# Local-and-global attention followed by a token and channel mixer: queries in nine blocks of 64, v loaded uncast and kept twice, PSUM banks handed out singly, and engine orders made by a list scheduler inside the kernel

## The chip, the cores and the metric

The kernel runs on one core of one Trainium2 chip. The metric is the device time of one execution in microseconds (us), lower is better. The engines are TensorE (PE, with its weight loads shown apart as PEld), VectorE (DVE), ScalarE (ACT), GpSimd (POOL) and SyncE (SP). DMAs are issued from the queues of SP, ACT and POOL. Each engine runs its instructions in the order in which the program lists them, and waits on semaphores where an instruction needs another engine's result.

## The reference

Eight batches, eight heads, 576 positions, head dimension 64. Attention is allowed within 32 positions, and to and from 8 global positions. The result, laid out as 576 x 512 for each batch, goes through two mixers with residuals.

```python
# attention: q, k, v are (8, 8, 576, 64) float32
scores = scale * np.matmul(q, k.transpose(0, 1, 3, 2))
mask = np.abs(pos[:, None] - pos[None, :]) <= 32
mask = mask | is_global[:, None] | is_global[None, :]
attn = softmax(np.where(mask, scores, -1e9))
x = (attn @ v).transpose(0, 2, 1, 3).reshape(B, S, 512)
# mixer: w_tok1 (576, 256), w_tok2 (256, 576), w_ch1 (512, 1536), w_ch2 (1536, 512)
h = relu(x.transpose(0, 2, 1) @ w_tok1) @ w_tok2
u = x + h.transpose(0, 2, 1)
out = u + relu(u @ w_ch1) @ w_ch2
```

## The kernel before

**What a batch does.** q and k are loaded as float32 (`lq`, `lk`, the last 64 rows in `lr`), cast to float16 (`cast_qk`, L350, into `qk` and `rn`) and turned so that the head dimension lies on the partitions: in batch 0 by TensorE transposes (`T`, `TE`, L416 to L435), later by DMA transposes on SP's queue (`turn_rest`, `turn`, L363 to L370, into `rawr` and `raw`), after which VectorE puts the columns in order (`order`, L376). `S_` (L437) makes scores for two heads at a time (a "pair", four to a batch). Keys lie in five tiles of 128 that begin 32 positions early, and each key tile meets up to 192 queries and 16 columns for the global positions: 10 matmuls to a pair, two heads at a time in the upper and lower half of the array's rows, of 208 or 144 columns. ScalarE takes the exponential in three instructions a pair (L457, L466, L469), and VectorE multiplies with the mask `bandm` (`SM`, L471: one instruction of 160 elements, two of 1040).

`GK` and `OG` do the global rows, `PV` (L512) multiplies the weights with v in five tiles of 128 queries: for each half of the heads one matmul of 264 columns for the global keys and two of 66 columns for each head, since the queries of a tile meet two key tiles. VectorE divides (L548, L549). `M1` and `M2` are the token mixer (results in `a1` and, with the residual, `u16`), `M3` turns u by DMA (L623, into `uT`), `M4` (L628) and `M5` (L653) are the channel mixer: twelve groups of four 512-column matmuls with a ReLU on ScalarE (L637, `b1`), then four tiles of twelve 512-column matmuls, a sum on VectorE (`osb`, L664) and the store. The last 64 rows of two batches share a tile and are done with the odd batch (`M4l`, `uTl`, L667).

**v.** Batch 0 loads v as float32 from SP and casts it on GpSimd (`castv`). All others load it with a DMA from GpSimd's queue that casts to float16 on the way (`load_v16`, L345). There is one copy, `vsh`, in key tiles of 128.

**PSUM.** Three pools hold the eight banks: two pairs of banks for scores, `GK`, `OG`, `M1` and `M2` (`pss`), one pair for `PV` (`psv`, so that a tile waits until VectorE has divided the one before), two single banks for the channel mixer (`psm`).

**Order.** The program is written under a manual schedule, so engines run what is written in its order. Batch 0 is written out by hand. After it `merge` interleaves two lists: the attention and token mixer of batch b+1 (`sparse`, L671) and the channel mixer of batch b (`dense`, L742), by hand-set weights in us:

```python
add(0.5, lambda p=p: S_(b, p, 0))
add(2.8, lambda p=p: S_(b, p, 1))
...
u = [(0.86, lambda j=j: M4(b, j)) for j in range(NJ)]
```

Of the kernel before, what the change touches and what calls it, by code (L numbers as in the profile page):

```python
# [15 lines left out]
P = 128  # L16
NT = 5
NG = 8
WIN = 32
GW = 2 * NG  # L20
QS = P + GW
EW = 2 * P + GW
VW = 66


def merge(sparse, dense):


    ts, td = sum(c for c, _ in sparse) or 1.0, sum(c for c, _ in dense) or 1.0
    i = j = 0  # L30
    a = d = 0.0
    while i < len(sparse) or j < len(dense):
        if j >= len(dense) or (i < len(sparse) and a / ts <= d / td):
            a += sparse[i][0]
            sparse[i][1]()
            i += 1
        else:
            d += dense[j][0]
            dense[j][1]()
            j += 1  # L40
# [3 lines left out]
def kernel(  # L44
# [24 lines left out]
    mb = ctx.enter_context(tc.tile_pool(name="mb", bufs=2))  # L69
    ob = ctx.enter_context(tc.tile_pool(name="ob", bufs=3))  # L70
    tiny = ctx.enter_context(tc.tile_pool(name="tiny", bufs=4))
# [6 lines left out]
    def pss(shape, dtype=F32, name="s"):  # L78
        return psS.tile(shape, dtype, tag="s", name=name)

    def psv(shape, dtype=F32, name="v"):
        return psV.tile(shape, dtype, tag="v", name=name)

    def psm(shape, dtype=F32, name="m"):
        return psM.tile(shape, dtype, tag="m", name=name)
# [4 lines left out]
    lv = mb.tile([P, NT, H, D], F32, tag="lv", bufs=1, name="lv")  # L90
    qk = const.tile([P, 2, NP, 4, P], F16, name="qk")
    rn = const.tile([P, NP, P], F16, name="rn")
    rawr = const.tile([P, NP, P], F16, name="rawr")
    vsh = [const.tile([P, NT, H, VW], F16, name=f"vsh{i}") for i in range(2)]

    gt32 = global_idx.tensor.bitcast(I32)
# [3 lines left out]
    nc.scalar.dma_start(out=gidx_b.rearrange("p g w -> p (g w)"), in_=bass.AP(tensor=gt32, offset=0, ap=[[0, P], [1, 2 * NG]]))  # L100

    def vrows(c):
        r0 = WIN if c == 0 else 0
        r1 = P - WIN if c == NT - 1 else P
        return r0, r1, P * c - WIN + r0

    def load_qk(b, hs):
        for ten, dst in ((q, lq), (k, lk)):
            nc.sync.dma_start(
                out=dst[:, hs].rearrange("p h i d -> p h (i d)"),  # L110
                in_=ten[b, hs, 0 : S - LAST, :].rearrange("h (p i) d -> p h (i d)", i=4),
            )

    def load_rest(b):
        for t, ten in enumerate((q, k)):
            nc.sync.dma_start(
                out=lr[LAST * t : LAST * t + LAST], in_=ten[b, :, S - LAST : S, :].rearrange("h p d -> p h d")
            )

    def load_v(b):  # L120
        for c in range(NT):
            r0, r1, j0 = vrows(c)
            nc.sync.dma_start(
                out=lv[r0:r1, c], in_=v[b, :, j0 : j0 + (r1 - r0), :].rearrange("h p d -> p h d")
            )

    for p in range(NP):
        load_qk(0, slice(2 * p, 2 * p + 2))
        if p == 0:
            load_rest(0)  # L130
    load_v(0)


# [263 lines left out]
    def G0(p):  # L397

        if p == 0:
            st[0]["pg"] = psm([P, NP, 2, NG], name="pg0")  # L400
# [457 lines left out]
```

## Time and profile before

| | us |
|---|---|
| time, median of 3 runs (lowest, highest) | 353.66 (353.2, 356.38) |
| span of the profiled execution | 353.0 |
| busy: PE, DVE, ACT, POOL | 299.4, 198.7, 163.3, 73.8 |
| HBM read | 36.12 MB, 129 GB/s over the span with 9.44 MB written |

The profiled execution's span is within 0.7 us of the median. A busy PE is not a PE at its peak: a matmul's row lasts longer than the distance to the next one, since they are pipelined. In the views a group's row gives line, engine, operation, tiles and shapes, the count after x, the busy time and the mean of one in ns, and behind the last bar the idle time of the engine ahead of them with what ended it.

### The profile page before, as it was taken

The numbers are of one execution on the slowest core, as the hardware profiler recorded it, in microseconds if no ns is written. First come the engines' busy times: TensorE is split into PE (matmuls) and PEld (weight loads), VectorE is DVE, ScalarE is ACT, GpSimd is POOL, SyncE is SP. The second block draws the span as 40 slices with busy tenths as digits, with TensorE's granted clock in tenths as the row PEclk, the third lists the DMA queues.
The fourth block names the chain that finished last, engine by engine and source line by source line (L and its number), as shares of the span: only waits on it lengthen the run. The fifth ranks groups of instructions, "written<-read, shape, count | busy, mean of one in ns | idle before, by whom it ended". The sixth has DMA issues, their size and how long they took to land.

```text
span 353.0 us, 6305 instructions
## 1 busy us (share of the span) xinstructions
PE 299.4 (85%) x2469; PEld 150.5 (43%) x2469; DVE 198.7 (56%) x407; ACT 163.3 (46%) x292; POOL 73.8 (21%) x113
## 2 busy tenths in 40 slices
PE   1556897893989896889899999798999998898994
PEld 0334433541337442454337434453366433543641
DVE  4898756657174583548545765568354946542021
ACT  2448279050582156806593339415870159012600
POOL 8888663100066200030002100130000000000000
PEclk9999999999799999999999999999999999999999
DMA  6999999996789997596659955595730240025012
GB/s 156 254 289 182 165 154 214 242 118 146 233 184 124 242 193 186 112 279 88 149 104 263 134 126 107 139 268 100 151 62 30 61 119 2 1 75 120 2 59 89
DMA packets 124317, 50.53 MB, mean 143 GB/s; under 512 B 99200, under 2 KB 119552, under 8 KB 124288
## 3 DMA queue, kind: packets, MB, share of 16 engines
q1 hardware_dynamic: 86800, 41.96, 52.1%
q0 software_dynamic: 37200, 8.16, 26.4%
q8 instruction: 19, 0.31, 0.4%
q14 instruction: 10, 0.08, 0.1%
q10 hardware_dynamic: 288, 0.01, 0.0%
HBM read 36.12 MB, written 9.44 MB: 129 GB/s over the span
## 4 chain that ended last, share of the span: by engine, by line
PE 58%; DVE 18%; DMA 9%; ACT 6%; SPq 5%; issue 2%; DVEq 0%; ACTq 0%
PE b1p L634 18%; PE op L660 18%; DMA uT<-u 5%; PE a1p L564 5%; SPq L623 4%; PE s L446 3%; PE pv L519 3%; DVE e_all L479 3%; PE pv L528 3%; DMA raw<-qk 2%; PE pv L533 2%; PE b1lp L647 2%; PE hp L588 2%; DVE x L549 2%; ACT e_all L457 2%
## 5 line engine op out<-in xcount | busy, mean ns | idle before, releaser
L634 PE MATMUL b1p<-uT,wc 128*128 128x512 f16 x384 | 94.5, 386 | 13.1 <-DMA uT<-u 11.3
L660 PE MATMUL op<-wc,b 128*128 128x512 f16 x384 | 90.5, 379 | 0.0
L637 ACT ACTIVATE b<-b1p 128x512 f16<-128x512 f32 x96 | 57.3, 614 | 37.7 <-PE b1p L634 36.2
L634 PEld LDWEIGHTS <-wc 128*128 128x128 f16 x384 | 33.9, 98 | 55.4 <-issue 19.1
L345 POOL DMA_DIRECT2D vsh<-in_v_dram x35 | 29.7, 855 | 115.3 <-PE pv L533 102.0
L660 PEld LDWEIGHTS <-b 128*128 128x128 f16 x384 | 36.2, 98 | 40.7
L457 ACT ACTIVATE e_all<-s 128x832 f16<-128x832 f32 x32 | 27.9, 872 | 38.0 <-PE s L446 25.1
L479 DVE TENSOR_TENSOR e_all<-e_all,bandm 128x1040 f16<-128x1040 f16 x64 | 43.8, 725 | 1.2
L664 DVE TENSOR_TENSOR osb<-u,op 128x512 f32<-128x512 f16 x32 | 21.8, 686 | 33.0 <-PE op L660 32.6
L473 DVE TENSOR_TENSOR eg<-e_all,bandm 128x160 f16<-128x160 f16 x32 | 8.1, 253 | 51.8 <-ACT e_all L469 51.8
L572 ACT ACTIVATE a<-a1p 128x1024 f16<-128x1024 f32 x7 | 7.2, 1024 | 59.5 <-PE a1p L564 59.0
L519 PE MATMUL pv<-rf,lf 128*128 128x264 f16 x80 | 21.5, 283 | 10.1 <-DVE x L549 5.2
L446 PE MATMUL s<-qT,kT 64*128 64x208 f16 (+1 forms) x320 | 23.8, 256 | 6.2 <-DVE qT L393 3.1
L549 DVE TENSOR_TENSOR x<-pv,rr 128x512 f16<-128x512 f32 (+1 forms) x40 | 27.6, 691 | 1.4
L528 PE MATMUL pv<-vsh,e_all 128*128 128x66 f16 x320 | 28.3, 197 | 0.0
L548 DVE RECIPROCAL rr<-pv 128x8 f32<-128x8 f32 (+1 forms) x40 | 8.3, 207 | 35.1 <-PE pv L533 23.7
L528 PEld LDWEIGHTS <-e_all 128*128 128x128 f16 x320 | 24.6, 100 | 4.2 <-issue 2.6
L533 PE MATMUL pv<-vsh,e_all 128*128 128x66 f16 x256 | 24.1, 198 | 0.0
L446 PEld LDWEIGHTS <-kT 64*128 64x128 f16 x320 | 10.8, 97 | 29.7 <-issue 21.7
L466 ACT ACTIVATE e_all<-s 128x576 f16<-128x576 f32 x32 | 21.0, 658 | 3.2 <-PE s L446 3.2
L356 ACT CAST qk<-lq 128x512 f16<-128x512 f32 x28 | 17.3, 618 | 5.4 <-DMA lq<-in_q_dram 5.3
L378 DVE COPY kT<-raw 128x512 f16<-128x512 f16 x28 | 16.7, 595 | 5.5 <-DMA raw<-qk 5.5
(154 smaller groups left out, 343.9 us busy)
## 6 DMA issues: line engine op xcount, KB each, us to landing
out_dram<-osb SPq DMA_DIRECT2D x32, 256.0 KB, 2.4
lq<-in_q_dram SPq DMA_DIRECT2D x7, 1024.0 KB, 6.5
lk<-in_k_dram SPq DMA_DIRECT2D x7, 1024.0 KB, 9.2
wc<-in_moe_w_ch_dram POOLq DMA_DIRECT2D x6, 512.0 KB, 9.9
vsh<-in_v_dram POOLq DMA_DIRECT2D x21, 128.0 KB, 9.5
vsh<-in_v_dram POOLq DMA_DIRECT2D x14, 96.0 KB, 5.4
lq<-in_q_dram SPq DMA_DIRECT2D x4, 256.0 KB, 5.9
lk<-in_k_dram SPq DMA_DIRECT2D x4, 256.0 KB, 5.8
```

The costliest lines, as they stand in the source:

```text
L345: nc.gpsimd.dma_start(out=vsh[b % 2][r0:r1, c, :, 0:D], in_=v[b, :, j0 : j0 + (r1 - r0), :].rearrange("h p d -> p h d"),)
L446: nc.tensor.matmul(ps[:, par, off : off + n], lhsT=kT[r, P * c : P * c + P], rhs=qf[r, lo : lo + n], start=True, stop=True,)
L457: nc.scalar.activation(out=e2[:, :, 1:3, 64:EW], in_=ps[:, :, 0 : 2 * W].rearrange("p h (c x) -> p h c x", c=2), func=AF.Exp, scale=scale)
L479: nc.vector.tensor_mul(out=eh, in0=eh, in1=bandm)
L519: nc.tensor.matmul(ps[:, hf, 0 : NP * VW], lhsT=s["lf"][:, P * tau - sh : P * tau - sh + P], rhs=s["rf"][:, 2 * hf : 2 * hf + 2], start=b ...
L528: nc.tensor.matmul(o, lhsT=e_all[:, h, tau, EW - P - sh : EW - sh], rhs=vsh[b % 2][:, tau, h, :], start=b == 0 and hh == 0, stop=last and ...
L533: nc.tensor.matmul(o, lhsT=e_all[:, h, tau + 1, 0:P], rhs=vsh[b % 2][:, tau + 1, h, :], start=False, stop=last)
L549: nc.vector.tensor_tensor(out=x16s[b % 2][r, tau, :].rearrange("p (f h x) -> p f h x", f=2, h=NP), in0=pq[r, :, :, 0:D], in1=rr[r].unsquee ...
L634: nc.tensor.matmul(ps, lhsT=wc1[:, cc, P * j : P * j + P], rhs=s["uT"][:, cc, :], start=(cc == 0), stop=(cc == 3))
L637: nc.scalar.activation(out=s["b1"][:, j, :], in_=ps, func=AF.Relu)
L660: nc.tensor.matmul(ps, lhsT=w, rhs=wc2[:, j, :], start=(j == 0), stop=(j == NJ - 1))
L664: nc.vector.tensor_add(out=osb, in0=s["u16"][:, tau], in1=ps)
```

## The change

The kernel is largely rewritten. The arithmetic stays the same; what changes is how the attention is cut, who casts, and who decides order and banks.

- **Blocks of 64 (`scores`).** Keys lie in nine blocks of 128 that begin every 64 positions; each block meets just the 64 queries in its middle and 8 global columns: 18 matmuls a pair, each of 72 columns, the two heads again in the two halves of the rows. One exponential for a head (9 x 72 elements), two a pair; one mask multiplication a pair (18 x 72), and one copy of the global columns into `eg`.
- **v.** Loaded as float32 in all batches and cast on GpSimd (`cast_v`). A second copy `vod`, shifted by 64 rows, is made from `vsh` by VectorE copies (`shift_v`), so that odd blocks find their 128 keys in one tile. `PV` (now `values`) keeps its counts.
- **Loads.** k of batch 0 is issued from ACT's queue. From batch 2 on q, k and v are all issued from GpSimd's queue.
- **Turns.** Batches 0 to 2 (`PEB = 3`) turn q, k and u on TensorE, with the evacuation on VectorE or ScalarE; later ones by DMA as before.
- **PSUM.** One tile `bank` of eight banks. Single results take any free bank, scores and `values` an even pair.
- **ReLU** may go to ScalarE or VectorE.
- **Order.** Every step is registered with `op`: engines it may run on with a cost in us, a priority, what it reads and writes. `run` is a list scheduler: it keeps a time for each engine, takes among the ready steps those that start first, and of those within a small look-ahead the one with the lowest priority number. `merge`, `sparse` and `dense` are gone. A function that fills PE's gaps with idle matmuls (`warm`) is there, but is called with a limit of 0.0, which gives none.

```diff
-    psS = ctx.enter_context(tc.tile_pool(name="psS", bufs=2, space=bass.MemoryType.PSUM))
-    psV = ctx.enter_context(tc.tile_pool(name="psV", bufs=1, space=bass.MemoryType.PSUM))
-    psM = ctx.enter_context(tc.tile_pool(name="psM", bufs=2, space=bass.MemoryType.PSUM))
+    bank = psum.tile([P, 8, 512], F32, name="bank")
...
+    def run(free, look, hop, warm_until):
...
+        while ready:
+            cand = {}
+            for i in ready:
...
+                for k, (e, c) in enumerate(o["opts"]):
+                    st = max([free[e], t0] + [f + (hop if x != e else 0.0) for x, f in at[i].items()])
...
+            for e, cs in cand.items():
+                lim = min(x[0] for x in cs) + look[e]
+                x = min((x for x in cs if x[0] <= lim), key=lambda x: (x[1], x[0], x[2]))
...
+            o["fn"](e)
...
+    def scores(b, p, pri):
...
+            for u in range(NB):
+                for z in range(2):
+                    r = slice(64 * z, 64 * z + 64)
+                    nc.tensor.matmul(
+                        ps_tile[keys[z]][:, u // 3, UW * (u % 3) : UW * (u % 3) + UW], lhsT=kT[r, 64 * u : 64 * u + P],
+                        rhs=qT[r, u // 2, UW * (u % 2) : UW * (u % 2) + UW], start=True, stop=True,
+                    )
...
+            op([("A", 0.73)], pri + 1, lambda e, par=par: nc.scalar.activation(
...
+        op([("V", 0.93)], pri + 2, lambda e: nc.vector.tensor_mul(
...
+    def chan1(b, j, pri):
...
+        op([("P", 0.865)], pri, f, r=[("wc1", j // 4)] + [("uT", t) for t in range(4)], ps=[key], new=("M", [key], [P, 512], F32))
+        op([("A", 0.61), ("V", 0.69)], pri - 8, lambda e: relu(e, b1[:, j, :], ps_tile[key]), ps=[key], w=[("b1", j)])
...
-            nc.gpsimd.dma_start(
-                out=vsh[b % 2][r0:r1, c, :, 0:D],
-                in_=v[b, :, j0 : j0 + (r1 - r0), :].rearrange("h p d -> p h d"),
-            )
+                    COPY[e](out=vsh[i][a:z, c, :, 0:D], in_=lv[a:z, c])
...
+                    if lo == 0:
+                        COPY[e](out=vod[i][0:64, cs], in_=vsh[i][64:P, cs])
+                    else:
+                        COPY[e](out=vod[i][64:P, cs], in_=vsh[i][0:64, cs.start + 1 : cs.stop + 1])
...
+    PEB = 3
...
+            gate = [start_of[b - 2]] if b >= 2 else []
```

The scheduler's result is what moves on the engines. Three places follow; a row is line, operation, result<-operands and shape, and x is a repeat.

**ScalarE, the exponentials of one batch beside the ReLUs of the batch before it** (`e_all` is the exponentials' output, `b` the ReLU's, `s`, `b1p` and `bank` are PSUM). Before, batch 6 beside batch 5:

```order
L457 ACTIVATE e_all<-s_6_0_2988 128x2x2x208
L637 ACTIVATE b_5_2994<-b1p_0_2995 128x512
L466 ACTIVATE e_all<-s_6_0_3001 128x2x2x144
L469 ACTIVATE e_all<-s_6_0_3001 128x2x208
L637 ACTIVATE b_5_2994<-b1p_1_3010 128x512
L637 ACTIVATE b_5_2994<-b1p_2_3016 128x512
L457 ACTIVATE e_all<-s_6_1_3025 128x2x2x208
L637 ACTIVATE b_5_2994<-b1p_3_3031 128x512
L466 ACTIVATE e_all<-s_6_1_3037 128x2x2x144
L469 ACTIVATE e_all<-s_6_1_3037 128x2x208
```

The same place now, from the first scores of batch 6 (`qk` is a cast for batch 7):

```order
L613 ACTIVATE e_all<-bank 128x9x72 x2
L637 ACTIVATE lf_82<-bank 128x512
L639 ACTIVATE lf_82<-bank 128x64
L769 ACTIVATE b_99<-bank 128x512 x2
L613 ACTIVATE e_all<-bank 128x9x72 x2
L473 CAST qk<-lq 128x2x4x64
L613 ACTIVATE e_all<-bank 128x9x72 x2
L473 CAST qk<-lq 128x2x4x64
L613 ACTIVATE e_all<-bank 128x9x72 x2
L769 ACTIVATE b_99<-bank 128x512 x3
```

Two exponentials stand where three stood, fewer ReLUs stand between them (27 of the program's 96 went to VectorE, whose row there is L771), and casts of the next batch have moved in.

**GpSimd's queue in later batches.** Before, two batches with just the loads of v, the cast in the DMA (`vsh_85` and `vsh_86` are the two buffers):

```order
L345 DMA vsh_85<-in_v_dram 96x8x64
L345 DMA vsh_85<-in_v_dram 128x8x64 x3
L345 DMA vsh_85<-in_v_dram 96x8x64
L345 DMA vsh_86<-in_v_dram 96x8x64
L345 DMA vsh_86<-in_v_dram 128x8x64 x3
L345 DMA vsh_86<-in_v_dram 96x8x64
```

Now, one batch: all its casts of v and, behind them, all loads of the next batch:

```order
L485 CAST vsh_76<-lv 32x8x64
L485 CAST vsh_76<-lv 64x8x64
L485 CAST vsh_76<-lv 128x8x64 x3
L485 CAST vsh_76<-lv 96x8x64
L453 DMA lr<-in_q_dram 64x8x64
L453 DMA lr<-in_k_dram 64x8x64
L443 DMA lq<-in_q_dram 128x8x256
L443 DMA lk<-in_k_dram 128x8x256
L462 DMA lv<-in_v_dram 96x8x64
L462 DMA lv<-in_v_dram 128x8x64 x3
L462 DMA lv<-in_v_dram 96x8x64
```

Five DMA issues a batch became nine and six casts, and the loads of q and k came over from SP.

**SP's queue, batch 1.** Before, its loads are followed by its nine DMA transposes:

```order
L116 DMA lr<-in_q_dram 64x8x64
L116 DMA lr<-in_k_dram 64x8x64
L109 DMA lq<-in_q_dram 128x8x256
L109 DMA lk<-in_k_dram 128x8x256
L364 DMA_TRANSPOSE rawr<-rn 128x4x128
L370 DMA_TRANSPOSE raw_497<-qk 128x4x128 x8
```

Now the loads come by pairs of heads, v behind them, and the first transpose by DMA is that of the shared last rows (`uTl`):

```order
L443 DMA lq<-in_q_dram 128x2x256
L443 DMA lk<-in_k_dram 128x2x256
L462 DMA lv<-in_v_dram 96x8x64
L462 DMA lv<-in_v_dram 128x8x64 x3
L462 DMA lv<-in_v_dram 96x8x64
L754 DMA_TRANSPOSE uTl<-ul_95 128x4x128
```

The transposes of batch 1's q and k moved from this queue to TensorE (32 + 4 of 128 columns).

More of the change, by code (lines that the diff above doesn't have):

```diff
@@ L20 @@
 GW = 2 * NG
+NB = 9
 QS = P + GW
-EW = 2 * P + GW
+UW = 64 + NG
+US = NG + P
 VW = 66
[L26 to L40, printed above, removed]
 @with_exitstack
@@ L96, with warm @@
+    zt = const.tile([P, 512], F16, name="zt")
+    nc.vector.memset(zt, 0.0)
+    def warm(n):
+        for _ in range(n):
+            nc.tensor.matmul(bank[:, 7, 0:256], lhsT=zt[:, 0:P], rhs=zt[:, 0:256], start=True, stop=True)
     gt32 = global_idx.tensor.bitcast(I32)
@@ L194 @@
     nc.vector.memset(kgz, 0.0)
[L195 to L200 removed]
+    nc.vector.memset(e_all[:, :, 0:NB:2, UW:], 0.0)
+    gpp = const.tile([P, 1], F32, name="gpp")
+    gpm = const.tile([P, 1], F32, name="gpm")
+    idx_i = const.tile([P, 4], I32, name="idx_i")
```

1272 lines of the change are left out of this document (685 added, 587 removed).

## The prediction

> **What bounds the kernel now.** I read the page first, then the busy time by stretches, then the chain that ended last, then the groups by line.
>
> ```profile
> span 353.0 us, 6305 instructions
> PE 299.4 (85%) x2469; PEld 150.5 (43%) x2469; DVE 198.7 (56%) x407; ACT 163.3 (46%) x292; POOL 73.8 (21%) x113
> PE   1556897893989896889899999798999998898994
> PEclk9999999999799999999999999999999999999999
> ```
>
> TensorE is busy for 85% of the span, at the full granted clock but for one slice. Its empty tenths lie in the first five slices; after that each slice misses little. So the loss is read by stage. I cut the span at the first channel product (L634) of each batch; the edges are the times at which the chain shows these matmuls.
>
> ```profile
> core 0: us, PE busy (x) PEld busy (x) DVE busy (x) ACT busy (x) POOL busy (x), PEclk, DMA share, GB/s
> 0.00:44.76 44.76, 24.97 (x268) 15.14 (x268) 33.57 (x95) 19.91 (x34) 35.46 (x70) 1.00 1.12 208
> 44.76:88.98 44.22, 33.81 (x273) 16.14 (x273) 27.83 (x59) 20.73 (x37) 10.37 (x9) 0.97 1.27 174
> 88.98:134.97 45.99, 40.52 (x328) 20.18 (x328) 26.22 (x48) 21.72 (x39) 15.41 (x19) 0.95 1.23 204
> 134.97:171.65 36.68, 32.65 (x267) 15.87 (x268) 22.20 (x42) 19.70 (x36) 4.20 (x5) 1.00 0.76 148
> 171.65:210.55 38.90, 38.17 (x327) 19.20 (x327) 22.77 (x43) 21.15 (x39) 4.21 (x5) 1.00 0.80 161
> 210.55:247.34 36.79, 32.67 (x267) 15.90 (x268) 22.20 (x42) 20.07 (x37) 4.20 (x5) 1.00 0.81 153
> 247.34:285.95 38.61, 38.16 (x327) 19.21 (x328) 22.62 (x43) 16.21 (x30) 0.00 (x0) 1.00 0.38 85
> 285.95:322.04 36.09, 32.30 (x263) 15.75 (x264) 17.83 (x32) 14.82 (x27) 0.00 (x0) 1.00 0.17 43
> 322.04:353.00 30.96, 26.19 (x156) 13.15 (x156) 3.44 (x5) 8.96 (x15) 0.00 (x0) 1.00 0.22 63
> ```
>
> Four kinds of stretch: 44.76 us until the channel mixer of batch 0 starts, with DVE busy for 33.57 and TensorE for 24.97; two slow batches (44.22 and 45.99); five settled ones, 36 to 39; and a tail of 30.96. The settled ones come in twos: batches in pairs share the last rows, so one stretch of two has more matmuls. Over the two stretches 171.65 to 247.34 TensorE is busy (38.17 + 32.67) / 2 = 35.4 us of 37.8 a batch.
>
> ```profile
> 46.84 8.80 DMA raw<-qk
> 169.08 2.48 DMA uT<-u
> 171.65 1.02 PE b1p L634 x4
> 322.04 10.56 PE b1p L634 x48
> 332.60 2.68 PE b1lp L647 x48
> 335.28 12.96 PE op L660 x60
> ```
>
> These pieces of the chain name what TensorE waits for: in batch 1 an 8.80 us piece of DMA transposes of q and k, later the transposes of u ahead of L634, as in the second and third piece. The last three are the tail's floor: a 512-column matmul follows the one before after 12.96 / 60 = 0.216 us, one of 128 columns after 2.68 / 48 = 0.056.
>
> ```profile
> L634 PE MATMUL b1p<-uT,wc 128*128 128x512 f16 x384 | 94.5, 386 | 13.1 <-DMA uT<-u 11.3 <-ACT b L637 1.4 <-issue 0.3
> L519 PE MATMUL pv<-rf,lf 128*128 128x264 f16 x80 | 21.5, 283 | 10.1 <-DVE x L549 5.2 <-DVE rf L506 4.6
> L637 ACT ACTIVATE b<-b1p 128x512 f16<-128x512 f32 x96 | 57.3, 614 | 37.7 <-PE b1p L634 36.2
> L457 ACT ACTIVATE e_all<-s 128x832 f16<-128x832 f32 x32 | 27.9, 872 | 38.0 <-PE s L446 25.1 <-issue 12.5 <-ACT b L637 0.4
> L466 ACT ACTIVATE e_all<-s 128x576 f16<-128x576 f32 x32 | 21.0, 658 | 3.2 <-PE s L446 3.2
> L469 ACT ACTIVATE e_all<-s 128x416 f16<-128x416 f32 x32 | 17.1, 534 | 0.0
> ```
>
> Three waits recur: u's transposes (11.3 us), the single bank pair of `PV`, which waits for the division (5.2), and ScalarE. While `M4` runs with the next batch's scores, ScalarE has 12 x 0.614 + 4 x (0.872 + 0.658 + 0.534) = 15.6 us of work by the means (a little less by the busy times, since neighbours overlap) for 48 x 0.216 = 10.4 us of `M4` and some 2.5 of scores.
>
> **The change part by part.** The 512- and 128-column products of the mixers keep their number: per pair of batches 96 + 108 + 20 + 20 of 512 columns, so none of TensorE's floor goes. What can go is idle time. I add up by milestones.
>
> *Start, now 44.76.* VectorE is the engine that works through it.
>
> ```profile
> L479 DVE TENSOR_TENSOR e_all<-e_all,bandm 128x1040 f16<-128x1040 f16 x64 | 43.8, 725 | 1.2
> L378 DVE COPY kT<-raw 128x512 f16<-128x512 f16 x28 | 16.7, 595 | 5.5 <-DMA raw<-qk 5.5
> 11.81 2.22 POOL L756 MEMSET e_all<- 128x2560 f16 x1
> 11.90 2.41 DVE L356 CAST qk<-lk 128x512 f16<-128x512 f32 x1
> 15.73 0.67 DVE L356 CAST qk<-lk 128x512 f16<-128x512 f32 x1
> ```
>
> It loses three of its four casts (two like the 0.67 and the one that took 2.41 beside GpSimd's memset of 2.22: 3.7 us), four of the eight large evacuations, which go to ScalarE (4 x 0.6 = 2.4) and, with the mask one instruction a pair, 4 x (2 x 0.725 - 0.725 x 1296/1040) = 4 x 0.55 = 2.2. The simpler masks save about 2 and the eight copies for `vod` cost about that (8 x 0.3, half a strided 0.595 copy, as they have half the lanes' work; an estimate). Together near 8 us off VectorE. What is late next is the weights:
>
> ```profile
> 22.89 0.80 POOL L231 DMA_DIRECT2D wc<-in_moe_w_ch_dram  x1
> wc<-in_moe_w_ch_dram POOLq DMA_DIRECT2D x6, 512.0 KB, 9.9
> ```
>
> The first third of `wc1` is issued at 22.89 and takes 9.9 to land. The new order puts the gathers ahead of it but drops the memset of 2.22, so I leave it there: 22.9 + 9.9 = 33, and I take **35** for the first channel product. Ends: 31, if only VectorE's relief and the earlier loads count, and 40, if half of it comes.
>
> *Batch 1, now 44.22.* Its q and k are turned on TensorE: 36 transposes at 0.056 are 2.0 us, 16 for u 0.9, and the 8.80 us wait for DMA transposes goes. Late next are the loads themselves, since batch 1's stand behind `wc1` and `wc2` behind both: 3.1 + 3.5 MB at the 208 GB/s of the first stretch are 32 us from 22.9 on, so the last of v lands near 55, and its casts, `values` and the token mixer follow before u can be turned. That just fits into TensorE's own 33.81 + 2.9 = 36.7 from 35 on, and I take **38**. Ends 35 and 43.
>
> *Six batches, now 322.04 - 88.98 = 233.1, or 38.8 each.* The settled floor is TensorE's 35.4. The order now puts four whole tiles of `M5` (48 x 0.216 = 10.4 us) behind `M2`, which cover u's sums and transposes (2.48 to land, 4 issues); `values` finds several free pairs of banks; ScalarE sheds 4 x (2.064 - 2 x 0.73) = 2.4 us a batch of exponentials (0.73 lies between the rows of 576 and 832 elements, for 648) and 27/96 of the ReLUs. I keep 0.6 for small waits: **36.0** each, and 2.9 for batch 2's transposes: 218.9. Ends: 34.5 (busy time contains stretched rows) and 37.8 (nothing gained on the settled rate).
>
> *Scores.* Ten matmuls a pair become 18 of 72 columns.
>
> ```profile
> 174.75 0.35 PE L446 MATMUL s<-qT,kT 64*128 64x208 f16 x4
> 175.04 1.04 PE L634 MATMUL b1p<-uT,wc 128*128 128x512 f16 x4
> L446 PEld LDWEIGHTS <-kT 64*128 64x128 f16 x320 | 10.8, 97 | 29.7 <-issue 21.7 <-DVE qT L393 4.4 <-DVE qT L381 1.7
> ```
>
> Four of 208 columns take 0.29 until the next product starts, two heads side by side, so weights are hidden there and columns count: 9 blocks x 72 is 648 columns for each head, before 3 x 208 + 2 x 144 = 912. By columns they get cheaper, 0.2 us a pair of heads; by weight loads, 18 for 10, dearer. I put 0, and the dear end under the rivals. The Trainium skill, page "TensorE: Matmul & The Clock Gate", section "The mechanism", says that a weight load overlaps matmuls in flight only when its row group differs; the second load of each head has the row group of the first. By that rule the sum would be 342 rather than 326.
>
> *Tail, now 30.96.* 10.56 + 2.68 + 12.96 and the last sum and store, unchanged: **31**.
>
> *GpSimd beside VectorE.* The casts of v, six a batch, are new on GpSimd.
>
> ```profile
> L390 POOL CAST vsh<-lv 128x512 f16<-128x512 f32 x3 | 1.8, 614 | 1.2 <-DMA lv<-in_v_dram 1.2
> L345 POOL DMA_DIRECT2D vsh<-in_v_dram x35 | 29.7, 855 | 115.3 <-PE pv L533 102.0 <-PE pv L528 6.3 <-DMA g_q<-in_q_dram,idx_i 2.7
> ```
>
> 6 x 0.614 = 3.7 us a batch, and four more DMA issues, 3.4. That a neighbour there can hold VectorE is shown by the cast of 2.41 against 0.67. VectorE has room (its work stays near 200 us by the rows above: 64 masks of 0.725 become 32 of 0.9, 27 ReLUs and the `vod` copies come), so only what falls on the way from scores to u counts: **3** in all, ends 0 and 43 (7.1 x 6).
>
> Sum: 35 + 38 + 218.9 + 31 + 3 = 325.9 of the profiled execution; the median of the runs lies 0.7 above its span, so **326.6**.
>
> **The rivals.** *Fixed order, late transfers.* The order is set by costs written in the kernel; where a transfer or an engine is later than its cost, everything behind the waiting row on that engine stands. On VectorE copies that wait for DMA transposes stand between the divisions and u's sums, so a late transpose delays `M2`'s bank and u together. Then the settled rate stays 38.8 and only the start is gained: 35 + 38 + 233.1 + 31 + 0.7 = 338. Against it: the loads now have a whole batch of lead, and the queue of SP loses 18 transposes of q and k and eight of u.
>
> *Scores dearer.* If each weight load is exposed, a block takes 0.097 + 72 x 0.216 / 512 = 0.13 us, a pair of heads 9 x 0.13 = 1.15 against some 0.64 now (0.29 x 912 / 416): 32 x 0.5 = 16 us more, 342. Against it: the 0.29 for four, which leaves no room for two loads of 0.097 in a row and 2 x 208 columns (0.18).
>
> *GpSimd holds VectorE (slower).* The new 7.1 us of GpSimd's work a batch fall on VectorE, and VectorE's on GpSimd, while TensorE waits for masks, divisions and sums. If all 7.1 reach TensorE's path the period is 43.1: 35 + 38 + 6 x 43.1 + 2.9 + 31 + 0.7 = 366. It makes the kernel slower by over 1% from (357.2 - 0.7 - 322.9) / 6 = 5.6 us a batch on. For it: the row of 2.41. Against it: VectorE is busy for 22 of 37 us, and most of those casts stand a batch ahead. The Trainium skill, page "SBUF — State Buffer", section "Who interferes with whom", states it as a rule: a GpSimd instruction and a VectorE copy or cast in a fast mode exclude each other, and one with two SBUF operands is held by a GpSimd reader. The row of 2.41 agrees with that.
>
> **How the numbers follow.** Forecast 0.60, at 311 to 336 by the ends of its terms, which will hardly all fall on one side. Fixed order 0.15 (330 to 350). Dearer scores 0.10 (335 to 352). GpSimd against VectorE 0.15: 0.10 of it past 357.2, 0.03 within 1% and 0.02 below. A measurement of this kernel tells no change from about 1%, 350.1 to 357.2. Faster: 0.60 + 0.15 + 0.10 - 0.04 (the upper ends of the two middle rivals) + 0.02 = 0.83; the same 0.04 + 0.03 = 0.07; slower 0.10. The range leaves out the slow rival and a little below: 310 to 348.
>
> **What would show it.** The first channel product at about 35 and that of batch 1 near 73; after that about 36 us a batch with no wait for u's transposes ahead of it; exponentials of about 0.73; scores of a pair within 0.8 us; a wait of `values` for the division under 1 us a batch. VectorE rows well above their usual length beside GpSimd's casts would show the slow rival; first channel products still 38 us apart, with `u` or `uT` named as releaser, the fixed order. I am wrong above all if the weights land later than 40 us, or if the order's costs fit this chip badly.

## The result

| | before | changed |
|---|---|---|
| time, median of 4 runs beside each other (lowest, highest), us | 355.02 (353.2, 358.99) | 385.77 (380.63, 389.29) |
| ratio, 95% interval | | 1.0763 (1.0646 to 1.0880) |
| profiled execution: time, span, us | span 353.0 | 380.63, span 378.9 |
| mean granted clock of TensorE | 0.990 | 0.941 |

The changed kernel is 7.6% slower where 326.6 us, 8% faster, was forecast. Runs more than 1.5% above the fastest of the same kernel are left out of the ratios: two of these four (387.79 and 389.29 us, which leaves 380.63 and 383.75 with a mean of 382.2), three of the four of the first experiment below with the profiled one among them (358.87 to 360.68 us, which leaves 353.02), and some runs of others; the time given for an edited kernel below is the median of the runs that stay.

The page's head for the changed kernel, with busy times by engine and the same two of its rows in 40 slices:

```profile
span 378.9 us, 7104 instructions
PE 305.7 (81%) x2824; PEld 164.8 (43%) x2824; DVE 211.0 (56%) x435; ACT 145.0 (38%) x259; POOL 114.0 (30%) x173
PE   1548695799799389775999759990799999999994
PEclk9999998599999869989999969996699999999999
```

TensorE has 6 us more of busy time and 26 us more of span. Unlike before, the holes go on through slice 29, most of them with a lower granted clock in or behind them. From slice 30 on there are none until the last. The busy time by stretches, cut as before at the first channel product of each batch (now L777):

```profile
core 0: us, PE busy (x) PEld busy (x) DVE busy (x) ACT busy (x) POOL busy (x), PEclk, DMA share, GB/s
0.00:45.83 45.83, 23.75 (x296) 16.84 (x297) 31.45 (x93) 16.24 (x29) 30.47 (x66) 1.00 0.82 175
45.83:93.13 47.30, 40.73 (x406) 24.29 (x406) 32.31 (x65) 22.60 (x42) 28.27 (x39) 0.89 0.87 201
93.13:142.66 49.53, 39.13 (x377) 20.30 (x371) 30.03 (x56) 19.68 (x35) 19.49 (x26) 0.90 0.72 161
142.66:187.57 44.91, 36.34 (x336) 18.03 (x328) 25.20 (x48) 17.06 (x32) 11.88 (x15) 0.96 0.64 151
187.57:229.38 41.81, 35.11 (x336) 18.77 (x329) 22.65 (x44) 16.36 (x30) 13.58 (x15) 0.92 0.69 152
229.38:278.62 49.24, 36.93 (x318) 17.67 (x311) 24.56 (x46) 15.87 (x30) 10.34 (x13) 0.86 0.59 131
278.62:314.49 35.87, 34.86 (x373) 19.19 (x366) 23.76 (x47) 17.86 (x33) 0.00 (x0) 1.00 0.30 78
314.49:347.82 33.33, 32.54 (x267) 16.63 (x267) 16.95 (x32) 10.35 (x18) 0.00 (x0) 1.00 0.23 57
347.82:378.90 31.08, 26.33 (x157) 13.09 (x155) 4.12 (x6) 8.96 (x15) 0.00 (x0) 0.99 0.15 51
```

The last two batches (35.87, 33.33) have no loads beside them, as GpSimd's empty columns show, and run at the 36 us forecast or below it. The four ahead of them take 41.8 to 49.5. So what costs time goes away together with the loads. The waits, what waits for what, with the total, the times and the longest:

```profile
POOL lq L443 <- ACT qk L473: 88.0, 7, 25.8
DVE kT L590 <- DMA raw<-qk: 35.5, 6, 12.6
PE bank L806 <- DVE ul L748: 16.2, 2, 12.3
PE bank L806 <- DVE osb L814: 13.7, 2, 7.7
```

(The two rows of L806 are 29.9 us together; the expectations below say 37 us, which these rows don't give.) Read from below: TensorE stops in the second channel product (L806) for a sum on VectorE; VectorE stands in its copy out of the DMA transposes (L590) for the transfer; and the loads (L443) are released by ScalarE's casts (L473). One such stop, in the timeline (start, duration, engine, line, operation, and in brackets the idle time ahead and its cause):

```profile
238.96 7.51 SPq L582 DMA_TRANSPOSE raw<-qk  x5
241.73 0.89 POOL L443 DMA_DIRECT2D lq<-in_q_dram  x1 [21.10 <-ACT qk L473]
242.61 1.30 POOL L443 DMA_DIRECT2D lk<-in_k_dram  x1
243.90 4.21 POOL L462 DMA_DIRECT2D lv<-in_v_dram  x5
250.29 2.32 PE L738 MATMUL bank<-a,w 128*128 128x512 f16 x10
252.45 2.75 PE L806 MATMUL bank<-wc,b 128*128 128x512 f16 x12
262.58 0.81 DVE L590 COPY kT<-raw 128x512 f16<-128x512 f16 x1 [12.63 <-DMA raw<-qk]
263.30 1.00 DVE L593 COPY qT<-raw 128x512 f16<-128x512 f16 x1
264.23 2.47 DVE L745 TENSOR_TENSOR u<-x,bank 128x512 f16<-128x512 f16 x4
266.72 0.69 DVE L748 TENSOR_TENSOR ul<-x,bank 64x512 f16<-64x512 f16 x1
267.47 10.45 PE L806 MATMUL bank<-wc,b 128*128 128x512 f16 x36 [12.26 <-DVE ul L748]
277.85 0.47 PE L605 MATMUL bank<-qT,kT 64*128 64x72 f16 x18
278.25 0.41 PE L632 MATMUL bank<-qT,kgz 128*32 128x512 f16 x4
```

ScalarE's casts of q and k do two things at once: they give SyncE's queue its DMA transposes, and they free `lq` and `lk`, so that GpSimd's queue issues seven loads of the next batch among those transposes. The last transpose takes 18.32 us to land, by its piece of the chain that ended last (from the start of its issue):

```profile
244.23 18.32 DMA raw<-qk
```

The token mixer's results (L738) have been lying in PSUM since 252.6. The u sums that would free those banks (L745, L748) stand behind L590 in VectorE's order, and TensorE waits 12.26 us for a bank. After the stop its 36 products take 10.45 us, 0.290 each, where 0.216 is the full rate; the granted clock over them is 0.75.

**Where the forecast's sum went.** Forecast against measured: start 35 and 45.8 (+10.8), batch 1 38 and 47.3 (+9.3), six batches 218.9 and 347.82 - 93.13 = 254.7 (+35.8), tail 31 and 31.1, the term for GpSimd 3 and none (-3), and between span and time 0.7 and 1.7 (+1). That makes 326.6 + 54.0 = 380.6.

### The profile page after: what moved, and what is told of

Same layout as the page of the kernel before. It is cut to its first block, busy times and chain, and to the rows that moved or that the text cites. A ratio compares the mean times of both kernels' runs of the same rounds, so it can differ in the third digit from the quotient of the medians.

```text
span 378.9 us, 7104 instructions
## 1 busy us (share of the span) xinstructions
PE 305.7 (81%) x2824; PEld 164.8 (43%) x2824; DVE 211.0 (56%) x435; ACT 145.0 (38%) x259; POOL 114.0 (30%) x173
## 2 busy tenths in 40 slices
DMA packets 69473, 51.30 MB, mean 135 GB/s; under 512 B 51456, under 2 KB 59520, under 8 KB 69440
## 4 chain that ended last, share of the span: by engine, by line
PE 56%; DMA 19%; DVE 17%; ACT 3%; issue 2%; SPq 1%; ACTq 0%; DVEq 0%
PE bank L806 22%; PE bank L777 18%; DMA raw<-qk 17%; PE bank L721 3%; DVE e_all L618 2%; PE bank L738 2%; PE bank L665 2%; DVE vod L497 2%; PE bank L677 2%; DVE vod L495 2%; PE bank L683 2%; PE bank L605 2%; SPq L582 1%; DVE u L745 1%; PE bank L789 1%
## 5 line engine op out<-in xcount | busy, mean ns | idle before, releaser
L806 PE MATMUL bank<-wc,b 128*128 128x512 f16 x384 | 91.7, 400 | 29.9 <-DVE ul L748 16.2
L777 PE MATMUL bank<-uT,wc 128*128 128x512 f16 x384 | 90.9, 379 | 4.9 <-DVE b L771 2.6
L613 ACT ACTIVATE e_all<-bank 128x648 f16<-128x648 f32 x64 | 42.1, 723 | 105.1 <-PE bank L605 99.9
L806 PEld LDWEIGHTS <-b 128*128 128x128 f16 x384 | 38.9, 102 | 79.5 <-issue 39.8
L769 ACT ACTIVATE b<-bank 128x512 f16<-128x512 f32 x69 | 41.1, 604 | 64.1 <-PE bank L777 63.6
L777 PEld LDWEIGHTS <-wc 128*128 128x128 f16 x384 | 35.7, 97 | 45.9 <-issue 6.9
L485 POOL CAST vsh<-lv 128x512 f16<-128x512 f32 (+3 forms) x48 | 33.5, 705 | 40.1 <-DMA lv<-in_v_dram 27.5
L443 POOL DMA_DIRECT2D lq<-in_q_dram x9 | 7.6, 842 | 88.1 <-ACT qk L473 88.0
L618 DVE TENSOR_TENSOR e_all<-e_all,masku 128x1296 f16<-128x1296 f16 x32 | 27.2, 850 | 10.2 <-ACT e_all L613 9.9
L590 DVE COPY kT<-raw 128x512 f16<-128x512 f16 x20 | 12.7, 649 | 35.6 <-DMA raw<-qk 35.5
L771 DVE TENSOR_SCALAR b<-bank 128x512 f16<-128x512 f32 x27 | 18.6, 689 | 23.5 <-PE bank L777 23.3
L677 PE MATMUL bank<-vsh,e_all 128*128 128x66 f16 x320 | 30.6, 207 | 0.0
L462 POOL DMA_DIRECT2D lv<-in_v_dram x30 | 28.3, 950 | 1.4 <-issue 1.1
L707 DVE TENSOR_TENSOR x<-bank,rr 128x512 f16<-128x512 f32 (+1 forms) x40 | 27.6, 690 | 1.4
L683 PE MATMUL bank<-vod,e_all 128*128 128x66 f16 x256 | 25.8, 205 | 0.0
L745 DVE TENSOR_TENSOR u<-x,bank 128x512 f16<-128x512 f16 x32 | 19.8, 680 | 2.8 <-PE bank L738 2.8
L738 PE MATMUL bank<-a,w 128*128 128x512 f16 x80 | 19.5, 379 | 0.7 <-ACT a L725 0.5
## 6 DMA issues: line engine op xcount, KB each, us to landing
lk<-in_k_dram POOLq DMA_DIRECT2D x5, 1024.0 KB, 10.9
```

The costliest lines, as they stand in the source:

```text
L462: ENG[e].dma_start(out=lv[r0:r1, c], in_=v[b, :, j0 : j0 + (r1 - r0), :].rearrange("h p d -> p h d"))
L485: COPY[e](out=vsh[i][a:z, c, :, 0:D], in_=lv[a:z, c])
L613: op([("A", 0.73)], pri + 1, lambda e, par=par: nc.scalar.activation(out=e_all[:, 2 * p + par, :, 0:UW].rearrange("p (n u) x -> p n u x", ...
L618: op([("V", 0.93)], pri + 2, lambda e: nc.vector.tensor_mul(out=e2, in0=e2, in1=masku.unsqueeze(1).to_broadcast([P, 2, NB, UW])), r=["mask ...
L677: nc.tensor.matmul(o, lhsT=e[:, u + NG : u + US], rhs=vsh[i][:, tau, h, :], start=start and hh == 0, stop=last and tau == NT - 1,)
L683: nc.tensor.matmul(o, lhsT=e[:, u - 64 : u + 64], rhs=vod[i][:, tau, h, :], start=False, stop=last)
```

## The experiments

The theory: loads on GpSimd's queue make DMA transposes on SyncE's queue late (the *collision*), and VectorE's fixed order turns the lateness into stops of TensorE. Rivals: GpSimd's casts hold VectorE (the *port*); the scheduler's order alone.

**Transposes off the DMA engines.**

```diff
-    PEB = 3
+    PEB, TURN = 3, B + 1
...
-        if b < PEB:
+        if b < TURN:
             rest_pe(b, ca - 38)
...
-                turn_u(b, tau, ca + tau + 2, b < PEB)
+                turn_u(b, tau, ca + tau + 2, b < TURN)
```

> All q, k and u of batches 3 to 7 are turned by TensorE again (as in batches 0 to 2); loads and casts stay as in the changed kernel. Collision theory: the loads of the next batch, released by the casts, run beside the DMA transposes, these land 12 to 18 us after their issue, and VectorE's copies of them stand ahead of the sums that free PSUM banks. Without DMA transposes the long stops of TensorE ahead of L806 (37 us in all) go: batches 2 to 5 fall from 41.8 to 49.5 us each to about 39, some 3 us of transposes a batch come on top; 350 to 362 us. Port theory (GpSimd's v casts hold VectorE): the casts are still there, no gain, 378 us or more.

Measured: 353.0 us. The stops ahead of the second channel product are gone, though GpSimd's casts and loads run as before. Batches 2 to 5 take 40.4, 39.0, 36.7 and 38.5 us in the profiled run, and the six batches with the tail 260.7 us for 285.8. (The 220.0 us of the six batches alone, in the table below, is too short by some 10: the first four channel products of batch 7 stand 11 us ahead of the others in this order.) The port theory asked for 378 or more.

**The loads later.**

```diff
+                def hold2(e):
+                    nc.gpsimd.tensor_copy(out=scr2[:, 0:1], in_=kTs[i][:, NP - 1, WIN : WIN + 1])
+                    nc.gpsimd.tensor_copy(out=scr2[:, 1:2], in_=qTs[i][:, NP - 1, 0, NG : NG + 1])
+                gate = gate + [op([("G", 0.2)], pl - 1, hold2, r=[("kT", i, NP - 1), ("qT", i, NP - 1)], w=["hold2"])]
```

> From batch 4 on GpSimd's queue waits, ahead of a batch's loads, for the last copy of the batch before out of its DMA transposes, so that loads and transposes of q and k no longer overlap. Collision theory: the transposes of batches 3 to 6 land in 2.5 to 4 us instead of 12 to 18, the stops ahead of L806 fall from 37 us to under 15, batches 3 to 6 come to 36 to 39 us: 345 to 358 us. If lateness comes from the order alone (casts too late, not slow transposes) or from GpSimd's casts beside VectorE: landings or stops stay, 375 us or more.

Measured: 364.29 us (1.0240, 1.0187 to 1.0293), faster than the changed kernel, but less than forecast. The transposes of q and k are back at a median of 2.5 us (10.9 at most), and L806 has no wait left. The collision moved to the next transposes on SyncE's queue, those of u. A piece of the chain, and three rows of the timeline:

```profile
245.45 17.98 DMA uT<-u
```

```profile
241.04 5.70 SPq L764 DMA_TRANSPOSE uT<-u  x4
242.11 0.89 POOL L443 DMA_DIRECT2D lq<-in_q_dram  x1
263.56 2.72 PE L777 MATMUL bank<-uT,wc 128*128 128x512 f16 x6 [10.35 <-DMA uT<-u]
```

The loads, held until the copies of q and k were out, now began among u's transposes, and one of these took 17.98 us. The lateness follows the loads.

**The copies later.** VectorE's four kinds of copy in `turn_dma` get an `after`, the last u sum of one batch and the second output sum of the batch ahead of it:

```diff
+        late = [sums[b - 1, NT - 1], outs[b - 2, 1]]
...
-                in_=raw[:, 1, p].rearrange("p i x -> p x i")), r=[("raw", 1, p)], w=[("kT", i, p)])
+                in_=raw[:, 1, p].rearrange("p i x -> p x i")), r=[("raw", 1, p)], w=[("kT", i, p)], after=late)
```

> The collision stays, but VectorE's copies out of the DMA transposes are ordered behind the u sums of the batch before and the first two output sums of the batch before that. Collision theory with VectorE's fixed order as the second half: landings stay at 12 to 18 us, the stops ahead of L806 that wait for u's sums go, part of them comes back ahead of the scores (L605): 350 to 368 us. Order-alone theory: landing times do not matter, all of it goes, 340 to 348 us. Port theory: no change, 375 us or more.

Measured: 344.26 us, 0.9702 of the kernel before (0.9671 to 0.9734). The collision is untouched, as the landing of q's and k's 40 transposes shows (lowest, median, highest):

```profile
DMA to landing us min/median/max: 2.4/3.4/17.9
```

Yet no stop is left ahead of the second channel product, and the six settled batches take 215.2 us. That is the time that the order-alone theory gave (340 to 348), not the collision's (350 to 368): a late transpose costs next to nothing here as long as nothing but its own reader stands behind it, and hardly any of the loss came back ahead of the scores.

The same with the u sum alone in `late`:

> VectorE's copies out of the DMA transposes are ordered behind the u sums of the batch before alone, and may stand ahead of the output sums. If the wait of u's sums is the whole of the stops, the time is that of the run with both, 343 to 347 us. If the output sums share them (13.7 us of the waits ahead of the second channel product named an output sum), the stops ahead of that product stay in part: 352 to 365 us.

Measured: 357.95 us (1.0030, 0.9984 to 1.0076), as expected of shared stops. The waits of TensorE in that kernel (the product is L808 there, the output sum L816):

```profile
PE bank L808 <- DVE osb L816: 13.0, 2, 8.6
```

The u sums no longer appear; the output sums, which also free a bank, do.

**The casts of v cut short.** From batch 3 on each cast copies one element, so v of an earlier batch is used.

```diff
-                    COPY[e](out=vsh[i][a:z, c, :, 0:D], in_=lv[a:z, c])
+                    if b < PEB:
+                        COPY[e](out=vsh[i][a:z, c, :, 0:D], in_=lv[a:z, c])
+                    else:
+                        COPY[e](out=vsh[i][a:z, c, 0, 0:1], in_=lv[a:z, c, 0, 0:1])
```

> From batch 3 on GpSimd casts one element of each tile of v instead of all (v of an earlier batch is used again), with the same waits. Port theory: VectorE's work beside those casts becomes shorter and the stops go, at least 12 us faster than the changed kernel. Collision theory: loads and transposes overlap as before, within 6 us of the changed kernel (375 to 388 us), if anything a little faster because the loads of v are not held up by the casts.

Measured: 383.48 us in one run, six settled batches 254.0 for 254.7, the mask multiplication 851 ns for 850. The port theory falls: the engines' orders are those of the changed kernel but for a few rows, and the gain of at least 12 us isn't there.

**The queue itself.** One part of the change undone: loads from batch 2 on go out on SyncE's queue.

```diff
-            load_rest(b, pl, [("G", 0.9)], gate, late)
+            load_rest(b, pl, [("S", 0.9)], gate, late)
...
-            load_v(b, pl + 6, [("G", 0.9)], gate, late)
+            load_v(b, pl + 6, [("S", 0.9)], gate, late)
```

> The changed kernel with one part undone: q, k and v of batches 2 to 7 are loaded through SyncE's queue again, where the DMA transposes are issued too, so that a load stands behind or ahead of a transpose instead of beside it. Collision theory: the transposes of q and k land in 2.5 to 5 us, the stops ahead of the second channel product fall from 37 us to under 15, 345 to 360 us. If the queue does not matter because the 16 DMA engines are shared whatever queue the work comes from, landings stay long (over 8 us) wherever loads are in flight, and the time stays at 372 us or more.

Measured: 339.83 us, 0.9534 (0.9490 to 0.9579). Stretches of its batches 2 to 5, and the landing of q's and k's transposes in that kernel (lowest, median, highest):

```profile
89.41:126.56 37.15, 35.63 (x377) 19.67 (x371) 26.82 (x52) 20.16 (x36) 4.58 (x7) 1.00 0.80 188
126.56:162.51 35.95, 34.48 (x337) 17.77 (x329) 22.89 (x45) 18.25 (x34) 4.00 (x6) 1.00 0.56 131
162.51:198.01 35.50, 34.10 (x346) 18.99 (x346) 22.54 (x45) 19.04 (x35) 3.61 (x6) 1.00 0.73 170
198.01:238.05 40.04, 36.14 (x329) 18.14 (x329) 25.41 (x49) 17.17 (x31) 4.14 (x6) 0.96 0.68 166
```

```profile
DMA to landing us min/median/max: 2.4/2.5/4.2
```

In the changed kernel the same view has

```profile
DMA to landing us min/median/max: 2.4/3.8/16.1
```

The view counts from the start of an issue, and only transposes that the trace ties to a landing: 11 of 40 with the loads on SyncE's queue, 5 of 40 in the changed kernel. The 16.1 is an earlier one (113.79 to 129.90); the 18.32 of the chain isn't among the five. The fastest version below has 24 of 40 counted, 4.3 us at most. The bytes are the same (51.30 MB in all), and the six settled batches take 217.6 us, near the forecast's 218.9.

The edit changes two more things. The scheduler counts an issue as time on its queue, so the orders of all engines are made anew: from 90 us on about 0.7 of VectorE's sequence is that of the changed kernel. And the 21.2 MB of these loads go out in other packets: by the difference of the two traces' queue tables in 6144 from GpSimd's queue, 3.5 KB each, and in 47040 from SyncE's, 0.45 KB each. The first is settled by the reverse below, where the order is written by hand and stays. The second isn't: no run puts the loads on a second queue with small packets, ScalarE's for instance, so whether any second queue makes transposes late or only one with large packets stays open.

The reverse, the kernel before with q and k of batches 2 to 7 on GpSimd's queue:

```diff
-            nc.sync.dma_start(
+            (nc.sync if b < 2 else nc.gpsimd).dma_start(
                 out=dst[:, hs].rearrange("p h i d -> p h (i d)"),
...
```

> The kernel before with one part of the change alone: q and k of batches 2 to 7 are loaded through GpSimd's queue. Collision theory: its DMA transposes, 2.5 us now, land after 5 to 15 us where they meet a load, and with its order written by hand, too, TensorE waits: 362 to 380 us. If the list scheduler's order alone turns late transposes into stops, the landings grow and the time doesn't: 354 to 359 us. If the queue has nothing to do with it, neither moves.

Measured: 385.01 us, 1.0885 (1.0821 to 1.0949). Landing and the two largest waits of TensorE in that kernel:

```profile
DMA to landing us min/median/max: 2.4/7.7/13.9
```

```profile
PE b1p L634 <- DMA uT<-u: 27.7, 6, 10.0
PE s L446 <- DVE qT L393: 10.5, 2, 10.2
```

The view counts 28 of 56 transposes here; from batch 2 on, where the loads moved, the median is 7.4 us, 2.4 in the kernel before. L634 waited 11.3 us for u's transposes before. So the order written by hand is no shelter; it only has the wait elsewhere, ahead of M4. One caution: its loads of v stand on GpSimd's queue too, now behind those of q and k, and land after 9.5 to 18.0 us (3.4 to 12.8 before); but the waits that grew name transposes.

**With the loads on SyncE's queue, does the place of the copies still matter?** On top of the indices-first edit (below):

> The run before and VectorE's copies ordered behind the sums as well. If late transposes were all that made the place of the copies matter, nothing is left to gain once they land in 2.5 us, and 0 to 2 us may be lost ahead of the scores: 335 to 341 us. If the place of the copies costs something of its own, another 3 us or more are gained: under 334 us.

Measured: 335.85 us (0.9485, 0.9445 to 0.9526) against 337.05 (0.9490, 0.9419 to 0.9560) without it. No difference that these runs can tell: once transposes land in time, copies that stand ahead of the sums cost nothing measurable.

**The start.** Four edits: the indices first (on top of the copies ordered last, and again on top of the loads on SyncE's queue), batch 2's loads later, v's copies on ScalarE, and the gathers later. One trace doesn't tell the first channel product to 2 us: the changed kernel and the one with the copies behind the u sums have the same order up to it and reach it at 45.8 and 47.6 us.

```diff
+    nc.scalar.dma_start(out=gpp_i, ...)
+    nc.scalar.dma_start(out=gidx_b..., ...)
...
+        if b == 2:
+            gate = gate + [v_done[1]]
```

(The two index transfers now stand ahead of k on ScalarE's queue; in the second run the loads of batch 2 wait for v's casts of batch 1.)

> On top of the run with the copies ordered last (344.4 us): the two small transfers of the global indices are issued first on ScalarE's queue instead of behind and between the loads of k. If the wait for them (5.1 us on the chain of waits) sets the start, the gathers, the mask, the casts of v and the weights behind them on GpSimd's queue come 5 us earlier, the first channel product of batch 0 falls from 43.2 to 38 to 40 us and the time to 338 to 341 us. If the start is set by the loads and weights themselves, under 2 us are gained: 342 to 345 us.

Measured: 338.52 us (0.9521, 0.9445 to 0.9597). The time is the one expected, the reason isn't: the first channel product stays (44.0 for 43.2), and batch 1 is shorter (47.0 for 53.0). Batch 1 took 47.3 in the changed kernel and 53.1 with the casts cut short, though nothing was edited there, so one profile's 5 us in that stretch proves little.

> As the run before, and GpSimd's queue issues the loads of batch 2 only behind its casts of v of batch 1. With the copies last, v of batch 1 landed 19 us after its issue, beside loads of batch 2, and TensorE stood 14.6 us in pieces ahead of batch 1's global scores and values. If that overlap is what makes batch 1 long, its stage falls from 53 us to about 45: 330 to 335 us. If the weights ahead of v make it late anyway, or if batch 2 then waits for its own loads, 337 us or more.

Measured: 338.50 us (0.9487, 0.9428 to 0.9546). Batch 1 falls to 44.5 us and batches 2 and 3 rise from 38.6 and 38.1 to 42.0 and 40.2; nothing is left, as the second half of the expectation had it.

> The run with the loads back on SyncE's queue (339.8 us), and the two transfers of the indices first on ScalarE's queue. Transposes stay at 2.5 us. If the indices hold the start, the 4 us that they gave beside the copies ordered last come again: 335 to 337 us. If the settled batches no longer care and the start is set by VectorE and the weights, under 1 us: 339 to 340.5 us.

Measured: 337.05 us against 339.83; the intervals overlap.

```diff
-        shift_v(b, ca - 19, [("V", 0.3), ("G", 0.6)] if b < PEB else [("V", 1.1)], ...)
+        shift_v(b, ca - 19, [("A", 0.5)] if b == 0 else [("V", 0.3), ("G", 0.6)] if b < PEB else [("V", 1.1)], ...)
```

> As the run with the indices first, and the eight copies of v's second arrangement for batch 0 go to ScalarE. They take 4.1 us of VectorE between 21.6 and 30.0 us, where VectorE is busy for 9.55 of 10 us. If VectorE sets the start, the first channel product of batch 0 comes 3 to 4 us earlier and the time falls by as much: 332 to 334 us. If the weights or ScalarE set it, under 1 us: 335 to 338 us.

Measured: 335.37 us (0.9504, 0.9420 to 0.9588). The first product stays at 45.0. The copies now delay ScalarE's exponential of the global rows (27.75 us for 21.83), yet the products that wait for it begin earlier (29.08 for 31.00); behind them the first six products of `M2` take 2.46 us for 1.55, and the lead is gone. Batch 1 takes 41.8.

> The run with the loads on SyncE's queue and the indices first (337.1 us), and the four gathers of batches 1 to 3 behind the first weights on GpSimd's queue, as in the kernel before, instead of ahead of the mask, v's casts and the weights. If the gathers ahead hold the start (8.4 to 13.6 us of that queue, and a wait of 0.8 us for them), the casts of v come 4 to 5 us earlier, the first channel product falls from 44.5 to 40 to 42 us and the time to 333 to 335 us. If VectorE sets the start, neither moves: the first product stays within 1 us of 44.5 and the time is 336 to 338 us.

Measured: 337.62 us (0.9537, 0.9498 to 0.9576); first product 43.3, between the two expectations and within what single traces differ by. The gathers aren't shown to hold it.

**All together.**

> All together: loads on SyncE's queue, indices first, copies behind the sums, the second arrangement of v for batch 0 on ScalarE, gathers behind the first weights. If each start edit takes its own piece: first channel product at 38 to 41 us, 328 to 332 us. If they only hand the start from one engine to the next: 333 to 336 us, as with two of them alone.

Measured: 331.88 us (330.34 to 333.39 in six runs), 0.9355 of the kernel before (0.9318 to 0.9392), the fastest version here. Its head and first two stretches:

```profile
span 330.0 us, 7118 instructions
```

```profile
0.00:44.30 44.30, 22.24 (x295) 15.35 (x295) 26.55 (x82) 21.43 (x37) 29.76 (x68) 0.88 0.98 203
44.30:84.13 39.83, 37.65 (x408) 21.85 (x408) 29.96 (x67) 21.60 (x39) 15.51 (x25) 1.00 0.88 202
```

VectorE has 4.9 us less to do in the first stretch than in the changed kernel, and the first channel product comes only 1.5 us earlier.

The kernels side by side, cut at the first channel product of batch 0, batch 1 and batch 7 (us, one trace each; "time" is the median of the runs that stay, for the turns on TensorE one run, whose trace is of another):

| kernel | time | start | batch 1 | six batches |
|---|---|---|---|---|
| before | 355.0 | 44.8 | 44.2 | 233.1 |
| changed | 382.2 | 45.8 | 47.3 | 254.7 |
| forecast | 326.6 | 35 | 38 | 218.9 |
| casts of v cut short | 383.5 | 43.6 | 53.1 | 254.0 |
| loads held for the copies | 364.3 | 42.9 | 50.2 | 240.8 |
| turns on TensorE | 353.0 | 42.6 | 53.4 | 220.0 |
| copies behind the u sums | 358.0 | 47.6 | 47.4 | 231.2 |
| copies behind u and output sums | 344.3 | 43.2 | 53.0 | 215.2 |
| the same, indices first | 338.5 | 44.0 | 47.0 | 214.7 |
| the same, batch 2's loads later | 338.5 | 43.8 | 44.5 | 219.1 |
| loads on SyncE's queue | 339.8 | 44.3 | 45.1 | 217.6 |
| the same, indices first | 337.1 | 44.5 | 44.4 | 215.7 |
| the same, gathers late | 337.6 | 43.3 | 43.2 | 215.9 |
| indices first, v's copies on ScalarE | 335.4 | 45.0 | 41.8 | 215.5 |
| indices first, copies behind the sums | 335.9 | 43.7 | 43.6 | 215.0 |
| all together | 331.9 | 44.3 | 39.8 | 214.5 |
| before, q and k on GpSimd's queue | 385.0 | 45.0 | 47.1 | 257.9 |

## Why the prediction was wrong

**The step that failed** is in the six batches, the move of the loads to GpSimd's queue. The prediction never gave that move a price. It let q, k and u land in the 2.48 us that the kernel before shows, and set "the loads now have a whole batch of lead, and the queue of SP loses 18 transposes" against the rival of late transfers. But 2.48 us belonged to a kernel whose loads of q and k and whose transposes shared a queue and so came one behind the other. The lead was what did harm: the loads could start as soon as the casts freed their tiles, which is the very moment at which the transposes are issued. Undoing this one move takes 37.1 us out of the six batches, where 35.8 had been lost, and leaves 217.6 for the forecast 218.9; doing it alone to the kernel before, for q and k, costs 30.3 us (385.0 against 354.7 beside it). In the changed kernel the loss needs two things at once, late landings and copies that stand ahead of the sums: with the copies last and the landings as late as ever the six batches take 215.2. The terms beneath (four tiles of M5 as cover, free banks, fewer exponentials, TensorE's turns in batch 2) were right as a sum; no run takes them one by one.

The trace before had the warning in it. The landing of q's and k's transposes there is

```profile
DMA to landing us min/median/max: 2.4/2.5/13.0
```

and the 13.0 is in batch 1: its transposes are issued from 31 to 48 us, while GpSimd's queue is fetching weights and v, and the four of them that are counted land after 8.8 to 13.0 us. The prediction took the 8.80 us piece among them as a wait that goes when TensorE turns batch 1, and didn't ask what stood beside it.

The Trainium skill has the arbitration, page "DMA: Bandwidth & Descriptors", section "Queues, rings and completion order": each DMA engine goes round among the queues that have work, a packet from each in turn. The landings agree with that as far as they go: 18.3 us at most from two queues, 4.2 from one. The same page, section "Issuing engines are not separate DMA queues", says that issuing from several engines saves only the time of issue. For the kernel's time more than that was at stake here: the choice of queue moved one kernel by 42 us (382.2 to 339.8) and the other by 30.

**Start and batch 1** (20.1 us late). The forecast took 8 us off VectorE and put the weights next, at 33. VectorE's work in the start fell by 2.1 us (33.57 to 31.45). The first weights are issued at 28.37 us where the forecast left them at 22.89, but the first channel product waits for `uT` (0.68 us), not for them. What the sum had no term for is TensorE's own way from the masks to that product: the last of the global rows (L649), which wait for a VectorE copy, start at 28.70, and `values`, the token mixer and u's transposes follow one behind the other to 45.83, with TensorE busy for 13.29 of these 17.13 us. For 35, L649 would have had to start near 18. With all edits in, VectorE has 26.6 us and L649 starts at 24.92, 3.8 earlier, but the way from there takes 19.4 us and the product comes at 44.3. Why it became longer, and what made batch 1 late, is left open; batch 1's 38 was reached within 2 us (39.8) once all edits were in.

**Tail**: 31.1 for 31. **Exponentials**: 0.723 for 0.73. **The waits named**: L777 has no wait for u's DMA transposes, as forecast, and `values` waits for the division 4.6 us, all in one batch.

**The rivals.** *Fixed order, late transfers* had the mechanism, down to the copies between the divisions and u's sums, with a chance of 0.15. Its price was wrong: it kept the settled rate at 38.8, as if lateness could only eat the gain, and the rate became 254.7 / 6 = 42.4. An 18 us landing in a 36 us batch needed a slower end. *Scores dearer* fell: the 18 matmuls of a pair at 277.85 are followed by the next product 0.40 us later (0.30 or 0.40 in 16 of the 32 pairs), where the prediction had 0.64 for a pair before. By that row the rule on row groups in the Trainium skill, page "TensorE: Matmul & The Clock Gate", section "The mechanism", adds nothing here that could be told. *GpSimd holds VectorE* fell with the shortened casts: 383.5 us. The slowdown came, at 0.10, but not from there.

## What to carry to other kernels

A transfer's landing time is measured beside the transfers that it then met; when a change moves one of them to another queue, price the landing anew, with a slower end, and ask what the moved transfer is released by. Where an order is fixed, put instructions that wait for a transfer behind those that free a resource for the bottleneck engine: this alone was worth 38 us (382.2 to 344.3) with landings as late as ever, and nothing measurable once transfers were on time. An engine that is busy for nine tenths of a stretch is not thereby what sets its end: take work off it in a run before crediting the relief, and give the sum a term for what must still run behind it (17.1 us here).

## What the runs showed of the hardware

A DMA transpose of 128 KB within SBUF landed 2.5 us after its issue in the median and 4.2 us at most with a batch's 3.5 MB of loads in its own queue, and up to 18.3 us with the same loads in GpSimd's queue. The same loads are cut into packets of 3.5 KB by GpSimd's queue and of 0.45 KB by SyncE's. The stop of TensorE was paid for twice: the 36 products after the 12.26 us took 0.290 us each, at a granted clock of 0.75 over them, where 0.216 is the full rate, so 36 x 0.074 = 2.7 us more.
